# Attention feeding a gated feed-forward on one core: one pair's values moved next to another pair's scores

## The chip, the cores and the metric

The kernel runs on one core of one Trainium2 chip. The metric is the device time of one execution in microseconds (us); where several runs are given, their median stands with the lowest and the highest. A core has five engines, each with its own queue of instructions that it works off in order: TensorE (PE in the rows; PEld is its weight load), VectorE (DVE), ScalarE (ACT), GpSimd (POOL) and SyncE (SP, which here issues the DMAs). TensorE writes its results into PSUM banks of 128 partitions by 512 float32 columns, and VectorE and ScalarE read them from there.

## What is computed

The reference runs attention on 8 batches of 8 heads with 576 positions and 64 features, with a local mask for heads 0 to 3 and a strided mask for heads 4 to 7, and sends the result through a feed-forward without biases:

```python
scores = scale * np.matmul(q, k.transpose(0, 1, 3, 2))
scores = np.where(masks[None, :, :, :], scores, -1000000000.0)
scores = scores - np.max(scores, axis=-1, keepdims=True)
attn = np.exp(scores)
attn = attn / (np.sum(attn, axis=-1, keepdims=True) + 1e-09)
attn_out = np.matmul(attn, v)
x = attn_out.transpose(0, 2, 1, 3).reshape(B * S, H * D)      # 4608 x 512
h = x @ w_in                                                  # 512 x 2048
g = h * (1.0 / (1.0 + np.exp(-1.702 * h)))
return g @ w_out                                              # 2048 x 512
```

The local mask lets a position see the 32 positions up to itself, the strided one the earlier positions with the same remainder modulo 32.

## The kernel before, in words

**Pairs.** The attention of one batch is cut into six pairs (`_pairs`, line 57): three of kind `l` (local heads, 96 queries by 128 keys) and three of kind `s` (strided heads, up to 128 by 108), each pair holding two chunks of four heads. In the batches 1 and 2 they come in the order s, l, s, l, s, l. A pair goes through these steps, each a function that issues one or a few instructions:

- `scores` (line 215, TensorE): 48 small matmuls for `l`, 32 for `s`, into columns 0 to 255 of the two banks `s_banks` (both called `s` in the rows);
- `masked` (VectorE, out of the two banks into SBUF), `maxima` (VectorE), `below` (GpSimd, subtracts the maximum), `exps` (ScalarE), `totals` (VectorE, sum and reciprocal), `scaled` (GpSimd);
- `turn` (line 337): four transposes on TensorE into the first of the two banks, and one ScalarE copy, `kept`, to SBUF;
- `values` (line 341, TensorE): 48 or 32 small matmuls with the values, into the two banks from column `at` on (192 columns for `l`, 180 or 216 for `s`), and then `moves_of`/`moved` (ScalarE copies out of the two banks into the blocks of x: one per bank for `l`, two per bank for `s`);
- `load_qk` and `load_v` (SyncE) fetch the inputs of the pair two further on into the buffer that the pair has just left.

**Passes.** The first product (x times w_in) is done batch by batch. Pass 0 (batch 0) uses plain products: 64 units of six 128-column matmuls over 288 columns. From pass 1 on it uses seven products per weight block in place of eight (a Strassen-like scheme: `product`, `combine`, with sums of x blocks, `x_sum`, and of weight blocks, `t_sum`). Every float32 operand is split into a high and a low part (`x_high`/`x_low`, `w_high`/`w_low_part`, `t_high`/`t_low`), so a unit or product is six matmuls. In pass 0 the w_in blocks are also unpacked (`w_scale`, `w_low`, `w_high` on ScalarE, `w_join` and `w_low_part` on VectorE); in pass 1 the sums of weight blocks are made (`t_load` by DMA, `t_sum` on GpSimd, `t_high` on ScalarE, `t_low` on VectorE). After pass 7 the second product follows.

**Slots.** All order is written out by hand. The main loop counts slots; each slot holds one unit or product on TensorE (two where `product` of two blocks meet), and then whatever was put into that slot with `side(slot, function, ...)` (line 684). Functions of one slot run in the order in which they were registered. Every engine keeps program order, so the slot numbers fix the order of every queue; waits between engines follow from the data. `HEAD` is 61 (where pass 1 begins, `first(1)`), and a pass is 56 slots.

**The attention beside passes 0 and 1.** While pass b runs (b = 0 or 1), the six pairs of batch b+1 are spread over its slots (lines 742 to 752). Pair i begins at slot s = first(b) - 3b + 7i + 2 for b = 0 and without the 2 for b = 1, that is at 2, 9, 16, 23, 30, 37 and at 58, 65, 72, 79, 86, 93. Its `scores` and `masked` stand at s, `maxima` at s+1, `below` at s+2, and the other steps at s plus the entries of `t`:

```python
t = ((4, 5, 6, 11, 12) if b else (2, 3, 3, 10, 12)) if not i else (5, 6, 7, 10, 12)
# exps, totals, scaled, turn, values
```

So the values of pair i stand at s+12, two slots ahead of the scores of pair i+2 at s+14. From pass 2 on (`groups_of`) two pairs go together: the scores of both are written side by side into the two banks before the first of them is read, and so are the values of both.

**Weight sums for pass 1.** Lines 766 to 773 place the steps of weight block i relative to `HEAD`: for block 1 `t_sum` at slot 59, `t_high` at 65, `t_low` at 67. Block 1's sums are first used by the product in slot 70.

Of the kernel before, what the change touches and what calls it, by code (L numbers as in the profile page):

```python
# [31 lines left out]
PAIRS = 6  # L32
# [32 lines left out]
def _size(kind):  # L65

    return (QL, KL) if kind == "l" else (QS, KS)
# [3 lines left out]
def attn_ffn(ctx, tc, qk, vs, weights, masks, ident, out):  # L71
# [81 lines left out]
    s_banks = [psum.tile([P, 512], F32, name=f"s{j}") for j in range(2)]  # L153
# [8 lines left out]
    for j in (1, 2, 3, 0, 4, 5):  # L162
# [3 lines left out]
        t = prs[j].rearrange("p (i m) -> p i m", i=4)  # L166
# [34 lines left out]
    def windows(kind):  # L201

        if kind == "l":
            return [(BL * w, BL, BL * w, WL) for w in range(3)]
        return [(64 * w, 64, WS * w, WS) for w in range(2)]
# [135 lines left out]
    def values(p, banks, at=0):  # L341

        kind, b, c = pairs[p]
        nq = _size(kind)[0]
        v, pt = vts[p], pts[p % 2]
        n0 = QL if kind == "l" else RES[c] * NPOS
        for g in range(2):
            for w, (q0, n, _, nk) in enumerate(windows(kind)):
                if kind == "s":
                    n = min(n0, (w + 1) * WS) - w * WS  # L350
                for u in range(U):
                    i = U * g + u
                    o = g * n0 + (q0 if kind == "l" else w * WS)
                    for j in range(2):
                        slot = j ^ u
                        rows = slice(slot * D, slot * D + nk)
                        matmul(
                            banks[u][j * D : (j + 1) * D, at + o : at + o + n],
                            lhsT=v[rows, i, w, :], rhs=pt[rows, i * nq + q0 : i * nq + q0 + n],
                            start=True, stop=True,  # L360
                        )
        return lambda u, *how: moved(p, u, banks[u][:, at : at + 2 * n0], *how)

    def moves_of(moves):
        for u in range(U):
            for move in moves:
                move(u)

    def moved(p, u, src, copy=scalar.copy, some=(0, 1)):
        kind, _, c = pairs[p]  # L370
        x = {k: xr[k].rearrange("p (g n) -> p g n", g=2) for k in ("11", "12", "21", "22")}
        src = src.rearrange("p (g n) -> p g n", g=2)
        if kind == "l":
            h, o = divmod(c + u, 3)
            copy(out=x[("11", "21")[h]][:, :, o * QL : (o + 1) * QL], in_=src)
            return
        n, r0, half = RES[c], R0[c + u], NPOS // 2
        src = src.rearrange("p g (r t) -> p g t r", r=n)
        for k in some:
            o = x[("12", "22")[k]].rearrange("p g (t r) -> p g t r", r=STRIDE)[:, :, :, r0 : r0 + n]  # L380
            copy(out=o, in_=src[:, :, k * half : (k + 1) * half])
# [235 lines left out]
    def move(i, second, engine):  # L617
        copy = vector.tensor_copy if engine is vector else scalar.copy
        if pairs[i][0] == "l":
            moves[i](second, copy)  # L620
        else:
            for u in range(2):
                moves[i](u, copy, (second,))
# [60 lines left out]
    def side(s, f, *a):  # L684
        sides.setdefault(s, []).append((f, a))

    def first(b):
        return HEAD + PASS * (b - 1) if b else 0
# [16 lines left out]
    def groups_of(b, slots):  # L705

        for g in range(3):
            q, s, then = b * PAIRS + 2 * g, slots[g] + 3 * (g > 0), slots[g + 1]
            side(s, both_scores, q)
            for i in range(2):  # L710
                s += 2 * i * (g == 0)
                side(s + i, masked, q + i, s_banks, 256 * i)
                for f, d in (
                    (maxima, 0), (below, 0), (exps, 4), (totals, 5 + (i and g > 0)),
                    (scaled, 5 + (i and g > 0)),
                ):
                    side(s + d + i, f, q + i, s_banks)
                side(then - (3 - (g > 0), 1)[i], turn, q + i, s_banks[i])
            side(then, both_values, q)

    for b in range(B):
        at = first(b)
        if b == 1:
            for t, f, k in ((-11, x_sum, 1), (-10, x_sum, 3), (-9, x_sum, 2), (-6, x_high, 1),
                            (-5, x_low, 1), (-5, x_high, 4), (-4, x_low, 4), (-3, x_high, 0),
                            (-2, x_low, 0), (-1, x_high, 2), (0, x_low, 2), (1, x_sum, 4),
                            (2, x_high, 3), (3, x_low, 3), (4, x_high, 6), (5, x_low, 6),
                            (6, x_high, 5), (7, x_low, 5)):
                side(at + t, f, k, b)
        elif b:  # L730
            c = b == 2
            side(at - 10 - c, x_sum, 1, b)
            side(at - 9 - c, x_sum, 3, b)
            for k in range(7):
                t = at + 2 * k - 6 + (k == 1)
                side(t, x_high, k, b)
                side(t + 1, x_low, k, b)
            side(at - 4, x_sum, 2, b)
            side(at, x_sum, 4, b)
        if 1 < b < B - 1:  # L740
            groups_of(b + 1, [at + t for t in (3, 16, 30, 44)])
        for i in range(PAIRS if b < 2 else 0):
            p = (b + 1) * PAIRS + i
            s = at - 3 * b + 7 * i + 2 * (not b)
            t = ((4, 5, 6, 11, 12) if b else (2, 3, 3, 10, 12)) if not i else (5, 6, 7, 10, 12)
            side(s, scores, p, s_banks)
            side(s, load_qk, p + 2)
            for f, d in ((masked, 0), (maxima, 1), (below, 2), (exps, t[0]), (totals, t[1]), (scaled, t[2])):
                side(s + d, f, p, s_banks)
            side(s + t[3], turn, p, s_banks[0])  # L750
            side(s + t[4], lambda p=p: moves_of([values(p, s_banks)]))
            side(s + t[4], load_v, p + 2)

    def word(f, i):
        f(raws[i])
# [9 lines left out]
            side(at + t, f, i)  # L765
    for i in range(FP):
        load = -15 + i if i < 3 else 7 * i - 20
        sums, high, low = (-12, -4, -1) if not i else (7 * i - 10 + t + (i == 1) for t in (0, 6, 8))
        for m in range(4):
            side(HEAD + sums + (2 if i > 1 and m > 1 else 0), t_sum, i, m)  # L770
        for t, f in ((load, t_load), (high, t_high), (low, t_low)):
            side(HEAD + t, f, i)
# [241 lines left out]
    for n in range(SETS * NB):  # L1014
        s, q = divmod(n, NB)
# [126 lines left out]
```

## Time and profile before

| | before |
|---|---|
| median of 3 runs | 831.76 us (831.07 to 832.25) |
| the profiled execution, its own time | 831.36 us |
| its span, first to last instruction | 829.3 us |
| TensorE busy | 818.5 us (99%) |
| VectorE busy | 591.7 us (71%) |
| ScalarE busy | 416.3 us (50%) |
| GpSimd busy | 500.3 us (60%) |
| chain that ended last: TensorE's share | 82% |

The profiled execution took 2.06 us more than its span, and lies 0.40 us under the median of the runs. In the timeline a row is a start time in us from the span's start, a length in us, the engine, the operation with the tiles that it writes and reads, the shape, and the number of instructions merged into the row; in square brackets stands how long the engine sat idle before it and what it waited for. `arena` is the one large SBUF tile in which most blocks lie, `mx`, `my`, `mz` are the six product banks, `s` the two attention banks. Matmuls are pipelined: a row's length reaches into the next row, so the cost of a group is read from its start to the next group's start.

### The profile page before, as it was taken

How to read it: one execution, taken by the hardware profiler on the slowest of the kernel's cores; microseconds unless marked ns; L12 is line 12 of the kernel's file. 1: busy time of each engine (PE TensorE's matmuls, PEld its weight loads, DVE VectorE, ACT ScalarE, POOL GpSimd, SP SyncE). 2: the span in 40 equal slices, each digit the busy share in tenths (PEclk: the TensorE clock that was granted, in tenths of full speed). 3: DMA queues.
4: the chain of work that ended last, by engine and by line, in shares of the span. 5: the costliest groups of instructions: out<-in, count | busy, mean ns of one | idle time of the engine just before them, and what ended most of it. 6: DMA issues, size and time to landing. Idle time of an engine off the chain costs nothing.

```text
span 829.3 us, 22486 instructions
## 1 busy us (share of the span) xinstructions
PE 818.5 (99%) x9037; PEld 762.1 (92%) x9037; DVE 591.7 (71%) x998; ACT 416.3 (50%) x642; POOL 500.3 (60%) x507
## 2 busy tenths in 40 slices
PE   7999999999999999999999999999999999999998
PEld 5899999999999999999999998889888888898898
DVE  5776877866767658567667876777767776777774
ACT  4666644534444444343446566555555555555550
POOL 4322886433442433233445359999999888888880
DMA  9898775685776775866678954444444444444431
GB/s 340 308 402 314 223 247 182 193 279 191 234 234 198 240 245 173 274 201 225 212 240 245 301 179 127 128 150 131 150 147 134 151 131 132 147 129 127 128 106 48
DMA packets 112504, 164.74 MB, mean 199 GB/s; under 512 B 9744, under 2 KB 88336, under 8 KB 111504
## 3 DMA queue, kind: packets, MB, share of 16 engines
q1 hardware_dynamic: 112400, 163.31, 60.1%
q8 instruction: 71, 1.16, 0.6%
q14 instruction: 33, 0.27, 0.1%
HBM read 104.55 MB, written 58.72 MB: 197 GB/s over the span
## 4 chain that ended last, share of the span: by engine, by line
PE 82%; DVE 2%; POOL 2%; DMA 1%; issue 1%; ACT 1%; SPq 0%; POOLq 0%; DVEq 0%; ACTq 0%
PE my L87 26%; PE mx L87 22%; PE mz L87 20%; PE s L87 14%; POOL arena L87 2%; DMA arena<-stash 1%; DVE arena L87 1%; DVE xa L87 1%; ACT xa L87 0%; DVE ga L87 0%; DVE w L87 0%; SPq L87 0%; ACT arena L87 0%; DVE w_out L87 0%; POOLq L87 0%
## 5 line engine op out<-in xcount | busy, mean ns | idle before, releaser
L87 POOL TENSOR_TENSOR arena<-arena 128x256 f32<-128x256 f32 (+1 forms) x298 | 331.2, 1128 | 119.0 <-ACT arena L87 39.2
L87 DVE TENSOR_TENSOR xa<-arena,xa 128x576 fp32r<-128x576 f32 (+3 forms) x101 | 152.3, 1511 | 42.0 <-ACT xa L87 37.2
L87 PE MATMUL my<-xa,w 128*128 128x288 f32 x1128 | 180.5, 301 | 0.7 <-DVE w L87 0.4
L87 ACT CAST xa<-arena 128x576 fp32r<-128x576 f32 (+3 forms) x103 | 115.3, 1140 | 90.3 <-POOL arena L87 29.4
L87 PEld LDWEIGHTS my<-xa,w 128*128 128x128 f32 x1128 | 156.2, 188 | 3.7 <-DVE w L87 1.0
L87 DVE TENSOR_TENSOR arena<-my,arena 128x288 f32<-128x288 f32 (+1 forms) x224 | 97.6, 443 | 59.1 <-PE my L87 56.3
L87 ACT COPY arena<-mx 128x288 f32<-128x288 f32 (+3 forms) x163 | 55.8, 364 | 158.9 <-PE mx L87 100.4
L87 PE MATMUL mz<-xa,w 128*128 128x288 f32 x804 | 129.9, 298 | 0.0
L87 PE MATMUL mx<-xa,w 128*128 128x288 f32 x804 | 129.6, 298 | 0.0
L87 ACT ACTIVATE arena<-arena 128x1024 f32<-128x1024 f32 (+2 forms) x120 | 105.3, 877 | 41.5 <-POOL arena L87 19.6
L87 POOL TENSOR_TENSOR arena<-arena,nmax 128x432 f32<-128x432 f32 (+1 forms) x42 | 48.2, 1149 | 110.1 <-DVE nmax L87 102.5
L87 PEld LDWEIGHTS mx<-xa,w 128*128 128x128 f32 x804 | 112.9, 188 | 1.0 <-POOL xa L87 0.2
L87 PEld LDWEIGHTS mz<-xa,w 128*128 128x128 f32 x804 | 113.1, 188 | 0.5
L87 DVE TENSOR_TENSOR arena<-mz,arena 128x288 f32<-128x288 f32 (+1 forms) x168 | 73.8, 442 | 37.0 <-PE mz L87 33.0
L87 POOL TENSOR_TENSOR arena<-arena,rinv 96x512 f32<-96x512 f32 (+1 forms) x48 | 51.2, 1067 | 60.9 <-DVE rinv L87 40.8
L87 PE MATMUL mx<-w_out,xa 128*128 128x512 f32 (+1 forms) x378 | 72.2, 317 | 0.0
L87 PE MATMUL mz<-w_out,xa 128*128 128x512 f32 (+1 forms) x366 | 71.4, 321 | 0.0
L87 PE MATMUL my<-w_out,xa 128*128 128x512 f32 (+1 forms) x366 | 71.3, 320 | 0.0
L87 DVE TENSOR_TENSOR ga<-arena,ga 128x1792 fp32r<-128x1792 f32 (+1 forms) x25 | 55.2, 2209 | 20.4 <-ACT ga L87 16.5
L87 PE MATMUL s<-w_out,xa 128*128 128x512 f32 (+1 forms) x378 | 67.7, 321 | 0.0
L87 ACT CAST ga<-arena 128x1792 fp32r<-128x1792 f32 (+1 forms) x25 | 40.8, 1632 | 44.2 <-POOL arena L87 16.0
L87 PEld LDWEIGHTS s<-w_out,xa 128*128 128x128 f32 x378 | 54.9, 188 | 5.8
(81 smaller groups left out, 1092.0 us busy)
## 6 DMA issues: line engine op xcount, KB each, us to landing
hid<-arena SPq DMA_DIRECT2D x256, 144.0 KB, 3.2
arena<-hid SPq DMA_DIRECT2D x144, 256.0 KB, 3.3
arena<-qk SPq DMA_DIRECT2D x23, 448.0 KB, 5.0
arena<-qk SPq DMA_DIRECT2D x21, 472.0 KB, 5.7
arena<-vs SPq DMA_DIRECT2D x23, 384.0 KB, 4.3
out<-arena SPq DMA_DIRECT2D x34, 256.0 KB, 3.6
stage<-w_out SPq DMA_DIRECT2D x16, 512.0 KB, 4.3
raw<-w_in SPq DMA_DIRECT2D x7, 1024.0 KB, 8.9
```

Of the source, the lines that this page charges most:

```text
L87: ins = call(*args, **kw)
```

## The change

The values of the first four pairs of each of the two passes go from s+12 to s+14, the slot in which the scores of pair i+2 stand, and write the columns from 256 on instead of those from 0 on; `load_v` of the pair two further on goes along. As the list of slot s+14 got the values first, the order there is: values of pair i on TensorE, the ScalarE copies of these values, `load_v`, then the scores of pair i+2. The last two pairs of each pass keep s+12 (they also write from column 256 on).

Beside this, four groups of entries move. In pass 0 the first pair's `turn` goes one slot later (12 to 13). In pass 0 the last pair's `exps`, `totals` and `scaled` go from slots 42, 43, 44 to 41, 42, 42. In pass 1 the first pair's `totals` goes one slot later (63 to 64). For weight block 1 `t_sum` stays at slot 59, `t_high` goes from 65 to 61 and `t_low` from 67 to 64.

```diff
             s = at - 3 * b + 7 * i + 2 * (not b)
-            t = ((4, 5, 6, 11, 12) if b else (2, 3, 3, 10, 12)) if not i else (5, 6, 7, 10, 12)
+            t = ((4, 6, 6, 11, 12) if b else (2, 3, 3, 11, 12)) if not i else (4, 5, 5, 10, 12) if i == PAIRS - 1 and not b else (5, 6, 7, 10, 12)
             side(s, scores, p, s_banks)
             side(s, load_qk, p + 2)
...
             side(s + t[3], turn, p, s_banks[0])
-            side(s + t[4], lambda p=p: moves_of([values(p, s_banks)]))
-            side(s + t[4], load_v, p + 2)
+            then = s + t[4] + 2 * (i < 4)
+            side(then, lambda p=p: moves_of([values(p, s_banks, 256)]))
+            side(then, load_v, p + 2)
...
-        sums, high, low = (-12, -4, -1) if not i else (7 * i - 10 + t + (i == 1) for t in (0, 6, 8))
+        sums, high, low = ((-12, -4, -1), (-2, 0, 3))[i] if i < 2 else (7 * i - 10 + t for t in (0, 6, 8))
```

## Rows read from the trace of the kernel before

**Rows 1.** The page's busy line: time, share of the span, instructions.

```profile
PE 818.5 (99%) x9037; PEld 762.1 (92%) x9037; DVE 591.7 (71%) x998; ACT 416.3 (50%) x642; POOL 500.3 (60%) x507
```

**Rows 2.** Timeline of TensorE in pass 0, slots 21 to 25 (start, length, what).

```profile
47.96 0.90 PE L87 MATMUL s<-arena 64*64 64x32 f32 x48
48.79 1.06 PE L87 MATMUL my<-xa,w 128*128 128x288 f32 x6
49.69 0.95 PE L87 MATMUL mz<-xa,w 128*128 128x288 f32 x6
50.57 0.74 PE L87 MATMUL s<-arena 64*32 64x64 f32 x48
51.23 1.06 PE L87 MATMUL mx<-xa,w 128*128 128x288 f32 x6
52.13 0.95 PE L87 MATMUL my<-xa,w 128*128 128x288 f32 x6
52.92 0.95 PE L87 MATMUL mx<-xa,w 128*128 128x288 f32 x6
```

**Rows 3.** Timeline of TensorE's weight loads: rows with an idle time before them.

```profile
38.19 0.42 PEld L87 LDWEIGHTS s<-ident_sb,arena 128*128 128x128 f32 x4 [0.63 <-POOL arena L87]
...
76.53 0.36 PEld L87 LDWEIGHTS s<-ident_sb,arena 96*128 96x128 f32 x4 [0.70 <-POOL arena L87]
...
95.08 0.69 PEld L87 LDWEIGHTS my<-xa,w 128*128 128x128 f32 x5 [0.35 <-DVE xa L87]
98.69 0.56 PEld L87 LDWEIGHTS my<-xa,w 128*128 128x128 f32 x4 [0.64 <-DVE w L87]
...
101.81 0.56 PEld L87 LDWEIGHTS s<-arena 64*64 64x64 f32 x32 [0.16 <-issue]
```

**Rows 4.** Timeline of TensorE in pass 1: values of kind s, values of kind l.

```profile
99.42 0.69 PE L87 MATMUL s<-arena 54*64 54x54 f32 x32
100.03 1.06 PE L87 MATMUL my<-xa,w 128*128 128x288 f32 x6
...
106.94 0.90 PE L87 MATMUL s<-arena 64*64 64x32 f32 x48
```

**Rows 5.** Timeline of ScalarE: the copies that follow the values of rows 4.

```profile
100.14 0.71 ACT L87 COPY arena<-s 128x108 f32<-128x108 f32 x4 [1.50 <-PE s L87]
...
107.88 0.54 ACT L87 COPY arena<-s 128x192 f32<-128x192 f32 x2 [1.96 <-PE s L87]
```

**Rows 6.** Timeline of TensorE: the scores in slot 16 of pass 0.

```profile
42.79 0.69 PE L87 MATMUL s<-arena 64*64 64x54 f32 x32
```

**Rows 7.** Timeline of ScalarE in pass 0, slots 12 to 14.

```profile
38.93 0.59 ACT L87 COPY arena<-s 128x512 f32<-128x512 f32 x1 [1.39 <-PE s L87]
...
41.70 0.72 ACT L87 COPY arena<-s 128x108 f32<-128x108 f32 x4
...
42.80 1.16 ACT L87 ACTIVATE raw<-raw 128x1024 uint32<-128x1024 uint8 x1
```

**Rows 8.** Timeline of VectorE: w_join of slot 9; x_low of slot 64; t_low of block 1.

```profile
37.81 1.41 DVE L87 SCALAR_TENSOR_TENSOR raw<-raw 128x1024 uint32<-128x1024 uint32 x1
...
94.32 0.71 DVE L87 TENSOR_TENSOR xa<-arena,xa 128x576 fp32r<-128x576 f32 x1
...
97.43 1.21 DVE L87 TENSOR_TENSOR w<-sums,w 128x1024 fp32r<-128x1024 f32 x1
```

**Rows 9.** Timeline of GpSimd in pass 1, slots 64 to 67.

```profile
94.55 1.26 POOL L87 TENSOR_TENSOR arena<-arena,rinv 128x432 f32<-128x432 f32 x1 [1.88 <-ACT arena L87]
95.76 4.13 POOL L87 TENSOR_TENSOR sums<-sums 128x256 f32<-128x256 f32 x2
...
100.86 1.53 POOL L87 TENSOR_TENSOR sums<-sums 128x256 f32<-128x256 f32 x2
```

**Rows 10.** Timeline of ScalarE in pass 1, slots 71 and 72.

```profile
102.43 1.05 ACT L87 CAST w<-sums 128x1024 fp32r<-128x1024 f32 x1 [0.87 <-POOL sums L87]
103.39 0.39 ACT L87 COPY arena<-mx 128x288 f32<-128x288 f32 x1
```

## The prediction, made before the changed kernel ran

> **What bounds the kernel now.** I read the page's busy line first: TensorE is busy 818.5 us of the span, and every other engine under three quarters of it [rows 1]. So a microsecond that TensorE loses or wins in the passes 0 and 1 moves the end by about as much, and the question is what happens on TensorE's own line. There I read the timeline of the stretch that is edited. Between two plain groups the starts lie 0.79 us apart (52.13 to 52.92). A stretch of small attention matmuls breaks this twice: the group ahead of it takes 0.88 (49.69 to 50.57) and the group behind it 0.90 (51.23 to 52.13), so each separate stretch costs 0.09 + 0.11 = 0.20 us beside its own length, which is 0.83 for the values of kind l (47.96 to 48.79) and 0.66 for the scores (50.57 to 51.23) [rows 2]; 0.61 for the values of kind s (99.42 to 100.03) [rows 4]. Last, the weight loads that waited: TensorE stood at two `turn`s for GpSimd (slot 12 at 38.19, slot 47 at 76.53) and at two products for VectorE (slot 67 at 95.08, slot 70 at 98.69); the ordinary gap ahead of an attention stretch is 0.16 [rows 3].
>
> **The change part by part, and what it costs.** Sums are made against the profiled execution, 831.36 us, which lies 0.40 under the median of the runs shown; that difference is left alone.
>
> *Merging.* Eight values stretches (four pairs, two passes) lose their own entry and exit: 8 x 0.20 = -1.60 us. This is certain in itself: whatever happens between values and scores, TensorE goes to small matmuls once instead of twice.
>
> *The small moves.* `turn` one slot later in pass 0: the wait of 0.63 less the ordinary 0.16 goes, -0.47. The last pair's `exps`, `totals`, `scaled` earlier: the wait at 76.53 goes, 0.70 - 0.16 = -0.54; the weight unpacking that ScalarE and VectorE then do later is first used many slots on. In pass 1 `totals` goes behind the `x_low` of slot 64, which then runs earlier by about `totals`' length, so the 0.35 at 95.08 goes. `t_low` of block 1 three slots earlier removes the 0.64 at 98.69 [rows 3]. Sum -2.00. What these make late: the 0.71 us `x_low` now stands ahead of `totals`, and the 1.21 us `t_low` ahead of the next `masked` [rows 8], so `scaled` of slot 64 starts 0.7 later, and GpSimd with it; that is priced below, since it matters only there. `t_high` at slot 61 falls into a stretch in which ScalarE otherwise waits for GpSimd: 0.
>
> *`load_v` two slots later.* It is passed by a few stores and loads on SyncE's queue, it still waits only for the values, as before, and its buffer is next needed 14 slots (some 11 us at 0.79) later: 0.
>
> *The new wait.* This is where the sign is decided. In slot s+14 TensorE writes the values into columns from 256 on of the two banks, ScalarE copies them out, and the next TensorE instruction, the first score, writes columns 0 to 255 of the same two banks. Must it wait for the copies? Before the change two slots of products lay between, so the question never came up. The trace has no row in which TensorE writes one half of a bank while another engine reads the other half; wherever the kernel puts two pairs side by side in a bank (passes 2 and on), all matmuls into it come ahead of the first read. So the price lies between nothing and the full length of the copies. I take the full wait, because in all rows here a bank is written, read and written again in turns, as one tile `s` [rows 2, 4, 5], and column offsets alone are no evidence that the order is kept by columns.
>
> The Trainium skill (PSUM — Partial Sum Buffer, section "PSUM bank collisions raise a hardware error") says that two engines must be kept apart by bank and group of 32 partitions, not by address, and that disjoint columns of one bank still collide. By that the scores wait for the copies, as in my sum; without it the sum would end at the first rival's time. No run here shows it yet.
>
> Its least length, with ScalarE free: the copies begin 0.72 after the start of s values (99.42 to 100.14) and take 0.71, so the scores can start 1.43 after the values instead of 0.61: 0.82 us. For l they begin 0.94 after it (106.94 to 107.88) and take 0.54: 1.48 against 0.83, 0.65 us [rows 2, 4, 5]. Behind the waiting matmul stands all of TensorE's queue. Less the 0.20 for merging, a merge costs +0.62 (s) or +0.45 (l).
>
> *Where ScalarE is not free, pass 0, slot 16 (s).* ScalarE's queue ahead of the copies holds `w_high`, `kept`, `w_scale`, a product copy, `exps` and `w_low`. Before, this block ran from 38.93 to 42.80 + 1.16 = 43.96, with the old copies (0.72) in it [rows 7]: 4.31 without them. `w_high` now stands first and waits for `w_join`, which ends at 37.81 + 1.41 = 39.22 [rows 8], so the copies start at 43.53 and end at 44.25. The scores were at 42.79 [rows 6]; net +1.46 (0.47 and 0.20 already taken off: unwaited they would start at 42.12, so the wait is 2.13).
>
> *The other three of pass 0* (l, s, l): 0.45 + 0.62 + 0.45 = +1.52 at the least. The same `w_scale` and `w_low` stand ahead of them, but with the products that are now ahead of the values there is more time to work them off; if each were as bad as slot 16, 3 x (2.13 - 0.82) = 3.9 more. Nearest to free: I take +0.4.
>
> *Pass 1, slot 72 (s).* Ahead of the copies ScalarE has `t_high` of block 2 (slot 71), which waits for GpSimd's sums: before, 102.43 with 0.87 of waiting [rows 10], and no one on TensorE cared. Now TensorE waits through the copies for `t_high`, and so for GpSimd. GpSimd's block ran from 94.55 to 100.86 + 1.53 = 102.39 [rows 9] and shifts by the 0.71 of `x_low`: 103.10. Then `t_high` 1.05, a copy 0.39 [rows 10], the copies 0.71: 105.25, against scores at 101.81 [rows 3]: +3.44 net. The other bound: two of the sums took 4.13 and the two others 1.53 [rows 9]; if the first two ran as fast, 2.60 less: +0.84. The sums still run beside nearly the same VectorE work, with `t_low` taken out: nearer to the upper end, +2.70. (0.20, 0.35 and 0.64 are in these, as both ends go by GpSimd.) *The other three of pass 1*: GpSimd and ScalarE have caught up during that stall: +1.52.
>
> *Sum:* 1.46 + 1.52 + 0.40 - 0.54 + 2.70 + 1.52 = +7.06; 831.36 + 7.06 = 838.4 us. Later passes keep their order, and start later by as much.
>
> **Rivals.** *First, the other side: no wait.* If the order between engines goes by columns, the scores follow the values at once at all eight places, and what is left is -1.60 - 2.00 = -3.60: 827.8 us. It decides at one point, the gap between the last value and the first score in slot 16. For it: the offset 256 keeps the two column ranges apart, and the copies precede the scores only in the list. Against it: above. This is also the case in which the change does what it says, one stretch; in my forecast the stretch is cut in two by a wait.
>
> *Second, the wait at its least everywhere.* ScalarE's queue is worked off in time at slots 16 and 72 too. Then 8 merges are 4 x 0.62 + 4 x 0.45 = 4.28, and -2.00: 833.6 us. For it: ScalarE is busy only half of the span [rows 1]. Against: the two queues above are in program order, and their lengths come from rows.
>
> *Third, ScalarE late at all of pass 0.* The full 3.9 in place of 0.4, and 3.44 in place of 2.70: +11.3, 842.7 us. For it: the same weight unpacking recurs every seven slots. Against: two more products lie ahead.
>
> **How the numbers follow.** The forecast (wait by bank, long at slots 16 and 72) gets 0.72, with a range of its own from 836 to 841.5; no wait 0.12; least wait 0.08; late everywhere 0.05; 0.03 for effects that cancel within 0.2%. The range that holds the time 8 times in 10 reaches from 833.5, under the second rival, to 841.8, short of the third. About 0.2% (1.7 us) is what a measurement of this kernel can tell from no change: faster 0.12, same 0.03, slower 0.85.
>
> **What would show it.** Right: in the eight slots TensorE idles between values and scores, released by ScalarE, about 0.65 to 0.8 us in most, over 2 at 42 us and some 3 to 5 near 101 us, there with `t_high` waiting for GpSimd ahead of the copies; the four waits of TensorE named above are gone. Wrong: score matmuls that start within 0.1 us of the last value while ScalarE still copies (then the first rival), or idle times of one length (then the second). A time above 842 would mean that a wait was passed on to later slots, which I don't expect since later passes had no wait on TensorE to add to.

## The result, and the profile after

The changed kernel takes 840.5 us (median of 4 runs, 840.19 to 841.06), against 831.65 us for the kernel before in the same session (4 runs, 831.07 to 832.25): ratio 1.010, 95% interval 1.0085 to 1.0116. It is slower by 8.85 us. The prediction was 838.4, with a range from 833.5 to 841.8.

The profiled execution took 841.06 us with a span of 839.0, against 831.36 and 829.3 before: +9.70 us in both. From the page of the changed kernel, the busy line (compare [rows 1]) and the granted clock in 40 slices of some 21 us:

```profile
PE 820.9 (98%) x9032; PEld 765.5 (91%) x9037; DVE 593.0 (71%) x998; ACT 417.2 (50%) x642; POOL 498.1 (59%) x507
PEclk9999989999999999999999999999999999999999
```

TensorE's busy time grew by 2.4 us only; most of what the span gained is idle time of TensorE. And there is a dent in the clock in one slice. Where both came from is read off TensorE's own line, at instructions that both kernels have (start of the same instruction in both traces; "step" is the growth since the line above):

| at | before | after | shift | step | predicted |
|---|---|---|---|---|---|
| scores of slot 2 | 30.92 | 31.30 | +0.38 | +0.38 | 0 |
| group behind the scores of slot 16 | 43.41 | 45.33 | +1.92 | +1.54 | +1.46 |
| group behind the scores of slot 37 | 66.65 | 70.03 | +3.38 | +1.46 | +1.92 |
| values of slot 49 | 78.62 | 81.31 | +2.69 | -0.69 | -0.54 |
| scores of slot 65 | 93.10 | 96.17 | +3.07 | +0.38 | 0 |
| scores of slot 72 | 101.81 | 107.54 | +5.73 | +2.66 | +2.70 |
| group behind the scores of slot 79 | 110.22 | 119.43 | +9.21 | +3.48 | +0.45 |
| values of slot 105 | 136.92 | 147.23 | +10.31 | +1.10 | +1.07 |
| end of the span | 829.3 | 839.0 | +9.70 | -0.61 | 0 |

The last step comes from the later passes, where the shift stays between 10.1 and 10.4 up to 426 us, and where a wait of 0.4 us that the kernel before has, for VectorE's `ga` near 519 us, does not occur.

The weight loads of TensorE that waited in the changed kernel (compare [rows 3]); the brackets give the idle time ahead of the instruction and who ended it:

```profile
42.45 0.57 PEld L87 LDWEIGHTS mz<-xa,w 128*128 128x128 f32 x4 [1.42 <-DVE w L87]
...
44.41 0.86 PEld L87 LDWEIGHTS s<-arena 64*64 64x64 f32 x32 [0.67 <-ACT arena L87]
52.72 0.77 PEld L87 LDWEIGHTS s<-arena 64*32 64x32 f32 x48 [0.52 <-ACT arena L87]
60.89 0.81 PEld L87 LDWEIGHTS s<-arena 64*64 64x64 f32 x32 [0.59 <-ACT arena L87]
69.17 0.77 PEld L87 LDWEIGHTS s<-arena 64*32 64x32 f32 x48 [0.52 <-ACT arena L87]
...
92.15 0.69 PEld L87 LDWEIGHTS mx<-xa,w 128*128 128x128 f32 x5 [0.35 <-DVE xa L87]
...
100.40 0.42 PEld L87 LDWEIGHTS s<-ident_sb,arena 128*128 128x128 f32 x4 [0.36 <-POOL arena L87]
102.17 0.19 PEld L87 LDWEIGHTS my<-xa,w 128*128 128x128 f32 x1 [0.56 <-ACT arena L87]
102.77 0.70 PEld L87 LDWEIGHTS my<-xa,w 128*128 128x128 f32 x5 [0.41 <-DVE xa L87]
...
107.54 1.24 PEld L87 LDWEIGHTS s<-arena 64*64 64x64 f32 x32 [2.56 <-ACT arena L87]
118.57 0.77 PEld L87 LDWEIGHTS s<-arena 64*32 64x32 f32 x48 [0.52 <-ACT arena L87]
126.83 0.81 PEld L87 LDWEIGHTS s<-arena 64*64 64x64 f32 x32 [0.67 <-ACT arena L87]
135.10 0.77 PEld L87 LDWEIGHTS s<-arena 64*32 64x32 f32 x48 [0.52 <-ACT arena L87]
```

Eight times the scores wait for ScalarE between the values and themselves, once for 2.56 us. The `turn`s of slots 13 and 47 and the products of slots 67 and 70 wait no longer. In their place others do: the product of slot 16, at 42.45, stands 1.42 us for `w_low_part` of VectorE, and there are waits at the product of slot 61 (92.15), the `turn` of slot 69 (100.40) and the product of slot 71 (102.17 and 102.77).

Two stretches of ScalarE's queue: the copies of the values of slot 16, and the queue ahead of the long wait (compare [rows 7] and [rows 10]):

```profile
43.96 0.71 ACT L87 COPY arena<-s 128x108 f32<-128x108 f32 x4
...
104.35 0.64 ACT L87 ACTIVATE arena<-arena 96x512 f32<-96x512 f32 x1 [2.66 <-POOL arena L87]
105.84 1.04 ACT L87 CAST w<-sums 128x1024 fp32r<-128x1024 f32 x1 [0.86 <-POOL sums L87]
...
107.09 0.71 ACT L87 COPY arena<-s 128x108 f32<-128x108 f32 x4
```

The values were written from 104.42 on, but their copies stand behind `exps` and `t_high`, which both waited for GpSimd. The copies end at 107.80; the scores start at 107.54 already, 0.26 earlier, which fits with the first of the two banks being free by then. TensorE after that wait, and the same stretch in windows (columns: busy time of the five engines, granted clock, share of DMA, GB/s):

```profile
104.42 0.69 PE L87 MATMUL s<-arena 54*64 54x54 f32 x32
107.54 1.42 PE L87 MATMUL s<-arena 64*64 64x54 f32 x32 [2.44 <-ACT arena L87]
108.89 1.81 PE L87 MATMUL mz<-xa,w 128*128 128x288 f32 x6
110.50 1.64 PE L87 MATMUL my<-xa,w 128*128 128x288 f32 x6
111.94 1.64 PE L87 MATMUL mx<-xa,w 128*128 128x288 f32 x6
```

```profile
104.00:108.00 4.00, 1.56 (x43) 1.25 (x44) 1.09 (x3) 2.58 (x7) 3.57 (x6) 0.89 0.65 201
108.00:112.00 4.00, 4.00 (x43) 3.90 (x44) 1.94 (x5) 0.00 (x0) 0.77 (x2) 0.50 0.70 217
112.00:116.00 4.00, 4.00 (x27) 3.98 (x27) 1.79 (x4) 2.21 (x4) 3.03 (x3) 0.76 0.13 47
```

The groups of products behind the wait start 1.61 and 1.44 us apart, where [rows 2] have 0.79 and 0.90: the granted clock is 0.50 there, which is the 1.2 GHz level. A row of this page that says "busy" does not say at which clock: in the window from 108 TensorE is busy all of its 4 us and does half the work.

### The profile page after: what moved, and what is told of

It reads as the page before. It is cut to its first block, busy times and chain, and to the rows that moved or that the text cites. A ratio compares the mean times of both kernels' runs of the same rounds, so it can differ in the third digit from the quotient of the medians.

```text
span 839.0 us, 22485 instructions
## 1 busy us (share of the span) xinstructions
PE 820.9 (98%) x9032; PEld 765.5 (91%) x9037; DVE 593.0 (71%) x998; ACT 417.2 (50%) x642; POOL 498.1 (59%) x507
## 4 chain that ended last, share of the span: by engine, by line
PE 84%; ACT 0%; DVE 0%; issue 0%
PE my L87 26%; PE mx L87 22%; PE mz L87 21%; PE s L87 15%; ACT arena L87 0%; DVE arena L87 0%
## 5 line engine op out<-in xcount | busy, mean ns | idle before, releaser
L87 POOL TENSOR_TENSOR arena<-arena,nmax 128x432 f32<-128x432 f32 (+1 forms) x42 | 50.7, 1208 | 122.4 <-DVE nmax L87 112.6
```

What stands on the lines that cost most here:

```text
L87: ins = call(*args, **kw)
```

## Experiments

Theory: the order between TensorE and the engine that empties a bank is kept by bank, so the scores wait for the copies of the values; the long wait at slot 72 also costs clock. Rivals: the column offset matters; the small moves matter; the time lies elsewhere in the moved values. The first four runs share 17 runs of the kernel before (median 832.26, 830.98 to 833.69), the last three another 17 (832.34, 830.94 to 836.08).

**Values in columns 0.** Edit of the changed kernel:

```
-            side(then, lambda p=p: moves_of([values(p, s_banks, 256)]))
+            side(then, lambda p=p: moves_of([values(p, s_banks, 0)]))
```

> The change with the moved values written from column 0 on in place of column 256, so over the columns that the next scores write; nothing else differs. Theory (the scores wait for the ScalarE copies because both touch the same bank, whatever the columns): the same time as the change, 840.5 us within 0.5, with the same waits of TensorE between values and scores. Rival (the offset of 256 columns buys something, as disjoint columns are ordered more loosely than overlapping ones): slower than the change, by 0.3 us or more at each of eight places, 843 us or above.

Measured: 842.12 us (840.69 to 843.06), ratio 1.0114 (1.0101 to 1.0128), which overlaps with the change's. TensorE's weight loads at slots 16 and 72, and its waits between 28 and 155 us (total, times, longest):

```profile
44.71 1.00 PEld L87 LDWEIGHTS s<-arena 64*64 64x64 f32 x32 [0.67 <-ACT arena L87]
...
109.37 0.85 PEld L87 LDWEIGHTS s<-arena 64*64 64x64 f32 x32 [2.56 <-ACT arena L87]
```

```profile
PE s L87 <- ACT arena L87: 5.6, 8, 2.4
```

The same eight waits to 0.01 us. With overlapping columns the wait must be there; with disjoint ones it is no shorter. So the order is not kept by columns, and the 256 buys nothing. Each of the two banks is one tile of the program, so no run here tells order by bank from order by tile.

The time is 1.6 us above the 840.5 of the theory, and under the 843 of the rival. The trace shows where the profiled execution lost more than the changed kernel's: the clock fell a second time, behind slot 16.

```profile
44.00:48.00 4.00, 3.46 (x53) 3.10 (x46) 2.22 (x6) 1.11 (x6) 1.04 (x1) 0.67 1.08 382
```

From the scores of slot 16 to the values of slot 23 it takes 8.53 us (44.71 to 53.24), in the changed kernel 7.00 (44.41 to 51.41, clock 1.00); behind slot 72 it is 8.52 against 9.73. From the scores of slot 2 to the values of slot 105 that makes 116.27 us (31.59 to 147.86) against 115.93, and the 0.34 between them is the clock's (1.53 less 1.21).

**The copies taken out from between.** ScalarE's copies are put behind the scores and `masked`; VectorE reads one column of each bank where they stood:

```
+            side(s, masked, p, s_banks)
+            if i > 1:
+                side(s, lambda p=p - 2: moves_of([held.pop(p)]))
...
+            if i < 4:
+                side(then, lambda p=p: held.update({p: values(p, s_banks, 256)}))
+                for bank in s_banks:
+                    side(then, lambda x=bank[:, 256:257]: vector.tensor_copy(out=warm, in_=x))
```

> The change with the ScalarE copies of the four moved pairs put behind the scores and masked of the same slot, and in their former place, between values and scores, one VectorE copy of a single column (256) of each of the two banks. Theory (order by bank: the scores wait for whatever reads the bank ahead of them): the scores now wait for VectorE, 0.2 to 0.4 us in each of the eight places, none waits for ScalarE, the 2.56 us wait in slot 72 is gone with the low clock behind it, and the copies in turn wait for masked, which only reads other columns of the bank; 832 to 834 us. Rival (the scores wait for ScalarE's work itself, for instance for its whole queue, not for a reader of the bank): waits on ScalarE stay, 839 us or more.

Measured: 836.7 us (836.26 to 838.59), ratio 1.0056 (1.0043 to 1.0068). Better than the change by nearly half of what it costs, but 2.7 us above the upper end of what was expected. Two weight loads of TensorE, and the first of ScalarE's copies:

```profile
52.39 0.81 PEld L87 LDWEIGHTS s<-arena 64*32 64x32 f32 x48 [0.36 <-DVE warm L87]
...
105.38 0.81 PEld L87 LDWEIGHTS s<-arena 64*64 64x64 f32 x32 [1.04 <-DVE warm L87]
```

```profile
45.81 0.72 ACT L87 COPY arena<-s 128x108 f32<-128x108 f32 x4 [1.58 <-DVE arena L87]
```

TensorE now waits for a read of one column by another engine, though the scores go to none of the columns that are read. Between values and scores no wait for ScalarE is left, and the clock is 1.00 throughout. What the expectation missed: 0.36 to 0.38 us remain in seven places, 1.04 at slot 72, where VectorE comes later to its read, and the 1.41 for `w_low_part` at 42.62 stays. A second thing shows: at seven of the eight places ScalarE stands idle 1.5 to 2.1 us ahead of its copies (columns from 256), until `masked` (columns below 256) by the releaser in the rows: two readers of one bank. To leave nothing at all between values and scores wasn't tried.

**Only the small moves.** The changed kernel with the values where they were before:

```
-            then = s + t[4] + 2 * (i < 4)
-            side(then, lambda p=p: moves_of([values(p, s_banks, 256)]))
+            then = s + t[4]
+            side(then, lambda p=p: moves_of([values(p, s_banks)]))
```

> The values, their columns and load_v as before the change; only the small moves (turn in pass 0, totals in pass 1, exps, totals and scaled of the last pair, t_high and t_low of block 1) are made. Theory of the prediction: their four waits go and nothing else comes, 2.0 us less than before, 829.6 us. Rival (the wait of 1.42 us for VectorE's low weight part that the change shows in slot 16, and the one of 0.36 us for GpSimd in slot 69, are what two of these moves turn into): 1.0 to 1.5 us less than before, 830.2 to 830.7 us.

Measured: 831.43 us (830.68 to 833.72, 12 runs), ratio 0.9993 (0.9985 to 1.0002): by the ratio 0.6 us less, and by the interval from 1.2 less to 0.2 more. The theory's 2.0 lies outside, and of the rival's 1.0 to 1.5 the interval touches only the lower end. TensorE's weight loads:

```profile
42.92 0.56 PEld L87 LDWEIGHTS s<-arena 54*64 54x64 f32 x32 [1.25 <-ACT arena L87]
...
66.75 0.79 PEld L87 LDWEIGHTS s<-arena 64*64 64x64 f32 x48 [1.09 <-ACT arena L87]
```

The old waits at slots 12, 47, 67 and 70 [rows 3] are gone. Four others stand: these two, and two that the changed kernel has as well, at slots 61 and 69 (0.35 at 92.16, 0.36 at 100.40). The first belongs to this experiment alone: `turn` comes a slot later and the values that need it stay where they were, so of the 1.25 some 1.09 (less the ordinary 0.16) don't speak of the change, and neither does that part of the time. The second, at the values of slot 35 (0.21 before, at 63.37), comes from a DMA that ScalarE waits for, as in the last experiment. This execution opened 2.07 us late, at the scores of slot 2; from there to the values of slot 105 it takes 0.64 longer than the kernel before, so without the 1.09 some 0.45 shorter, and without the 0.88 more at slot 35 some 1.33. So this run alone does not settle what the moves are worth; the last two experiments say more.

**TensorE kept at work in the long wait.** Fourteen extra 128x320 matmuls into a free bank, between values and scores of slot 72; their result is used nowhere:

```
+            if b == 1 and not i:
+                side(then, busy, 14)
```

> The change with 14 extra matmuls (128x128 by 320 columns, bfloat16, into a product bank that is free then; about 1.9 us of TensorE work) between values and scores of slot 72, where TensorE waits 2.56 us. Their result is not used. Theory (that idle time makes the clock fall to its lower level, which costs some 2.5 us in the products behind it): the granted clock stays at 1.0, the products after slot 72 start 0.79 us apart instead of 1.44 to 1.61, and the time falls by 2 to 2.8 us to about 838 us although TensorE has more to do. Rival (the products there are slow for another reason, such as what VectorE and GpSimd do beside them): 840.5 to 841.5 us, with the products as slow as in the change.

Measured: 840.28 us (837.71 to 841.36), ratio 1.0087 (1.0072 to 1.0103). TensorE's timeline, and its waits between 424 and 560 us:

```profile
105.25 0.69 PE L87 MATMUL s<-arena 54*64 54x54 f32 x32
105.87 2.08 PE L87 MATMUL mz<-masks_sb 128*128 128x320 bf16 x14
108.38 0.98 PE L87 MATMUL s<-arena 64*64 64x54 f32 x32 [0.43 <-ACT arena L87]
109.29 1.06 PE L87 MATMUL mz<-xa,w 128*128 128x288 f32 x6
110.18 0.95 PE L87 MATMUL my<-xa,w 128*128 128x288 f32 x6
110.97 0.95 PE L87 MATMUL mx<-xa,w 128*128 128x288 f32 x6
```

```profile
PEld mz L87 <- DVE arena L87: 0.9, 1, 0.9
PEld my L87 <- DVE ga L87: 0.5, 1, 0.5
```

The scores still start 3.13 us behind the values (3.12 in the changed kernel), so the gap is as long; but the clock is 1.00 in all three windows from 104 to 116, the groups are 0.89 and 0.79 apart, and from the scores of slot 72 to the values of slot 79 it takes 7.02 us instead of 9.73: 2.71 us are the clock's. The time misses the 838 of the theory: only 0.2 us is left against the change in the medians, 1.1 by the two ratios, whose intervals overlap, and 1.84 against the run with columns 0 on the same chip. The trace shows one reason: this execution is 1.87 us ahead of the changed kernel's at the `turn` of slot 103 (143.33 against 145.20), though it opened 0.81 later, and then stands 0.9 and 0.5 us in two places that the changed kernel passes without waiting. So the clock's price is shown in the stretch; at the end of the kernel, with openings that differ by 2 us between executions, the medians don't settle how much of it is left.

**Slot 72 left as it was.** Only this one pair's values go back:

```
-            then = s + t[4] + 2 * (i < 4)
+            then = s + t[4] + 2 * (i < 4 and not (b and i == 0))
```

> The change, but the first pair of pass 1 keeps its values in slot 70 (columns from 256 on); the other seven pairs stay moved. Theory (this one place costs 3.4 us of waiting for GpSimd through ScalarE, and the fall of the clock behind it 1.5 to 2.7 us more): the wait of 2.56 us is gone, the granted clock stays at 1.0 after it, and the time lies 5 to 6.5 us under the change's, at a ratio of 1.003 to 1.005 to the kernel before. Rival (what waits there is late anyway, and is waited for at the next place, by turn of slot 69 or 75 or by the values of slot 79): at most 3 us under the change, a ratio above 1.006.

Measured: 836.86 us (836.2 to 840.19), ratio 1.0055 (1.0035 to 1.0074); the profiled span is 834.4, 4.6 shorter than the change's. TensorE's weight load at slot 79, and ScalarE's `t_high` ahead of the copies that it waits for:

```profile
113.46 0.77 PEld L87 LDWEIGHTS s<-arena 64*32 64x32 f32 x48 [1.47 <-ACT arena L87]
```

```profile
111.84 1.04 ACT L87 CAST w<-sums 128x1024 fp32r<-128x1024 f32 x1 [0.92 <-POOL sums L87]
```

One of eight merges, with the clock behind it, costs about half of all. The ratio lies between what the theory (at most 1.005) and the rival (above 1.006) asked for, since 0.95 us are passed on: the wait of slot 79 is 1.47 instead of 0.52, as GpSimd and ScalarE, which catch up in the changed kernel while TensorE stands, are late here. The clock is 1.00.

**Only the moved values.** The changed kernel with the small moves taken back:

```
-            t = ((4, 6, 6, 11, 12) if b else (2, 3, 3, 11, 12)) if not i else (4, 5, 5, 10, 12) if i == PAIRS - 1 and not b else (5, 6, 7, 10, 12)
+            t = ((4, 5, 6, 11, 12) if b else (2, 3, 3, 10, 12)) if not i else (5, 6, 7, 10, 12)
...
-        sums, high, low = ((-12, -4, -1), (-2, 0, 3))[i] if i < 2 else (7 * i - 10 + t for t in (0, 6, 8))
+        sums, high, low = (-12, -4, -1) if not i else (7 * i - 10 + t + (i == 1) for t in (0, 6, 8))
```

> The moved values, columns and load_v of the change, with every other entry as before the change (turn, totals, exps and scaled of the last pair, t_sum, t_high, t_low). Theory of the prediction (the small moves are worth 2.0 us in the change): 842.5 us, a ratio of 1.013. Rival (they are worth next to nothing there: turn's wait only moves to the weight part of slot 16, and behind slot 72 everything waits for GpSimd, which starts 0.7 us earlier without the later totals): 840 to 841.5 us, a ratio of 1.009 to 1.012, with a shorter wait in slot 72 than the change's 2.56 us.

Measured: 841.24 us (839.96 to 842.35), ratio 1.0099 (1.0079 to 1.0119): the change without its small moves is the change, as the rival had it. TensorE's weight loads:

```profile
38.45 0.42 PEld L87 LDWEIGHTS s<-ident_sb,arena 128*128 128x128 f32 x4 [0.64 <-POOL arena L87]
42.33 0.56 PEld L87 LDWEIGHTS mz<-xa,w 128*128 128x128 f32 x4 [0.82 <-DVE w L87]
...
101.79 1.37 PEld L87 LDWEIGHTS my<-xa,w 128*128 128x128 f32 x10 [0.64 <-DVE w L87]
...
107.23 1.24 PEld L87 LDWEIGHTS s<-arena 64*64 64x64 f32 x32 [2.56 <-ACT arena L87]
```

The waits at 38.45 and 42.33 together are 1.46; in the changed kernel the first is gone and the second is 1.42. From the scores of slot 2 to the values of slot 105 it takes 115.80 us (31.18 to 146.98), the changed kernel 115.93 (31.30 to 147.23), so the small moves give nothing inside the change. The 2.56 at slot 72 stays to the hundredth, and is not shorter as the rival expected, since the values come as much earlier as their copies. The scores there come 11.04 us behind those of slot 65 (96.19 to 107.23), against 11.37 in the changed kernel and 8.71 before: the merge at slot 72 costs 2.33 there, and the small moves add 0.33.

**Two of the small moves alone.** The kernel before, with the last pair's `exps`, `totals` and `scaled` earlier and `t_high` and `t_low` of block 1 earlier:

```
-            t = ((4, 5, 6, 11, 12) if b else (2, 3, 3, 10, 12)) if not i else (5, 6, 7, 10, 12)
+            t = ((4, 5, 6, 11, 12) if b else (2, 3, 3, 10, 12)) if not i else (4, 5, 5, 10, 12) if i == PAIRS - 1 and not b else (5, 6, 7, 10, 12)
...
-        sums, high, low = (-12, -4, -1) if not i else (7 * i - 10 + t + (i == 1) for t in (0, 6, 8))
+        sums, high, low = ((-12, -4, -1), (-2, 0, 3))[i] if i < 2 else (7 * i - 10 + t for t in (0, 6, 8))
```

> The kernel before with two of the small moves alone: exps, totals and scaled of the last pair of pass 0 earlier, t_high and t_low of block 1 earlier. Theory (these two remove waits of TensorE without putting another in their place, while later turn and later totals only trade one wait for another): TensorE's waits in slots 47 and 70 are gone, and 0.6 to 1.2 us less than before, a ratio of 0.9985 to 0.9993. Rival (the time won in slot 47 is lost again where pass 1 begins, on the weight sums that come by DMA): within 0.4 us of before.

Measured: 832.41 us (831.3 to 834.85, 12 runs), ratio 0.9999 (0.9988 to 1.0011). No gain, and none in the trace: 106.05 us from the scores of slot 2 to the values of slot 105 (32.30 to 138.35), against 106.00 before. TensorE's weight loads:

```profile
65.21 0.79 PEld L87 LDWEIGHTS s<-arena 64*64 64x64 f32 x48 [0.64 <-ACT arena L87]
90.61 0.69 PEld L87 LDWEIGHTS mx<-xa,w 128*128 128x128 f32 x5 [0.35 <-DVE xa L87]
...
101.62 0.69 PEld L87 LDWEIGHTS my<-xa,w 128*128 128x128 f32 x5 [0.48 <-DVE xa L87]
```

The old waits at slots 47 and 70 are gone, 1.18 in all (0.70 less 0.16, and 0.64); the last two of these rows, at slots 61 and 71, take 0.83 of it back. The first row, at slot 35, stands ahead of everything that this edit moves (slot 41 is the first), so it is not put there by the moves. It waits for `kept` behind `w_high` on ScalarE, and that for a DMA; here and before:

```profile
63.74 1.05 ACT L87 CAST w<-raw 128x1024 fp32r<-128x1024 f32 x1 [3.31 <-DMA plains<-raw]
```

```profile
61.90 1.05 ACT L87 CAST w<-raw 128x1024 fp32r<-128x1024 f32 x1 [2.90 <-DMA plains<-raw]
```

Without the 0.43 that it has more than before (0.64 against 0.21) this execution would be 0.38 shorter than the kernel before, which twelve runs can't tell from nothing. The rival's time came; its reason, the weight sums that come by DMA, accounts at most for the 0.35 at slot 61: `t_high` of block 0 stands 1.41 us for GpSimd's sums there (1.01 before), and `x_high` behind it.

None of the seven is faster than the kernel before by more than its measurement is uncertain.

## Why the prediction was right, and where it was off

The mechanism that decides the sign was right: TensorE waits for the copies at all eight places. The size was 2.1 us short in the medians (838.4 against 840.5), as a clock that falls behind the longest wait was not in the sum; step by step:

**The new wait: right, and shown.** Eight waits between values and scores, released by ScalarE, and none by columns: the run with columns 0 has the same ones. The Trainium skill (PSUM — Partial Sum Buffer, section "PSUM bank collisions raise a hardware error") says that disjoint columns of one bank still collide between engines; the waits of both runs agree with that order (0.52 to 2.56 us). Whether the chip itself would object without it, no run here shows: what the traces have is the wait of the program.

**Slot 72: right in place, in size partly by luck.** +2.66 against +2.70, and by the queue that was predicted: the copies behind `t_high`, that behind GpSimd's sums. GpSimd in the changed kernel (compare [rows 9]):

```profile
98.62 1.73 POOL L87 TENSOR_TENSOR arena<-arena,rinv 128x432 f32<-128x432 f32 x1 [2.86 <-DVE rinv L87]
100.31 3.00 POOL L87 TENSOR_TENSOR sums<-sums 128x256 f32<-128x256 f32 x2
...
104.28 1.53 POOL L87 TENSOR_TENSOR sums<-sums 128x256 f32<-128x256 f32 x2
```

The upper bound, 3.44, had GpSimd 0.71 later and the scores behind the end of the copies; 0.74 was taken off it for sums that run faster. In the trace GpSimd's sums end 9.64 us behind the scores of slot 65 (105.81 less 96.17), 9.29 before (102.39 less 93.10): 0.35 later, not 0.71. That is the balance of three parts: `scaled` starts 1.00 later (2.45 behind those scores, 1.45 before) and takes 0.47 longer, and the first two sums take 3.00 instead of 4.13. So the sums did run faster, by 1.13, but against a later start than forecast. And the scores start 1.73 behind the sums, not 2.15, as the rows of ScalarE's queue overlap a little and the scores don't wait for the end of the copies. 3.44 - 0.36 - 0.42 = 2.66. That these parts come to what a choice between two bounds had taken off is luck. The idle time in the row is 2.56, under the "3 to 5" that it named: TensorE had by then waited itself, at the `turn` of slot 69 and the product of slot 71 (0.36, 0.56 and 0.41).

**Slot 16: right in sum, wrong in kind.** +1.54 against +1.46. ScalarE's queue came out as worked out: copies that end at 44.25, and 0.38 of the opening, make 44.63; the row has 43.96 + 0.71 = 44.67. But the wait is not one of 2.13 for ScalarE: 1.42 of it is ahead of the values, for VectorE's `w_low_part`, and 0.67 behind them. The prediction did not follow VectorE's queue, where `w_low_part` had been covered by the wait at `turn` and by the values that stood ahead of the product: with `turn` in its old place and only the values moved, 0.82 of the 1.42 is there.

**The other six: right.** 1.46 in pass 0 against 1.52 (the 0.40 on top did not come); in pass 1 1.10 for two and, by the like one in pass 0, 0.43 for the third, against 1.52. Each is made up of two parts that were not foreseen: the scores start 1.31 behind l values (51.41 to 52.72) and not 1.48, and then take 0.86 (52.72 to 53.58) and not 0.66; that they wait inside for the second bank fits with it, but no row shows it by itself.

**The small moves, -2.00: wrong.** Taken out of the change they cost nothing (1.0099 against 1.010, and 115.80 us against 115.93 for the stretch), and two of them on the kernel before gain nothing that twelve runs can show. All of them alone give 0.6 us by the ratio (1.2 less to 0.2 more), with 1.09 lost at slot 14 in that run only. The failed step is "the wait goes, less 0.16": the prediction asked what is late next for the moved instructions, not for the consumers behind the wait. The four waits are gone, and in the changed kernel 1.42 at slot 16, 0.35 at 61, 0.36 at 69 and 0.56 and 0.41 at 71 stand instead. Only -0.69 at slot 49 came as forecast (-0.54), and 0.38 of it went again at slot 61, where `x_high` waits behind `t_high` of block 0. As the queues of ScalarE and GpSimd set the steps at slots 16 and 72 anyway, little of this error reached the sum.

**The merging, -1.60:** not measured by itself; it is inside the steps above.

**The clock: missing.** Of the 3.48 us up to slot 79, 2.71 are the clock after the long wait, as the filled wait shows; the other 0.77 stand in that run too (0.43 the merge, the rest mostly the longer scores of slot 72, 0.91 instead of 0.62). That is the term by which the sum (+7.06 against +9.70) fell short, together with 0.38 at the opening, which lies in the spread of executions, and 0.38 at slot 61; a later gain of 0.61 and the 0.46 less at the merges of pass 0 go the other way.

## What to carry to other kernels

Before a producer is put next to another user of the same PSUM bank, look at what lies between: two slots of products had hidden the emptying of the bank, and disjoint columns do not replace them. Follow then the queue of the engine that empties it, back to whatever that engine waits for; this found the place of the longest wait, and bounds for its size, before it was there. And a short wait on the engine that bounds the kernel is worth its length only if the next consumers of the same chain have slack: read their start against their inputs' ends before counting it as gained.

## What was not expected of the hardware

A wait of 2.4 us on TensorE (1.56 us of work between 104 and 108) was followed by a granted clock of 0.50 from 108 to 112 and 0.76 from 112 to 116, though TensorE was busy in all of these 8 us. It cost 2.7 us in the profiled execution of the change, and 1.5 in that with columns 0 (8.52 us for the stretch, clock 0.78 and 0.80); in that of the moved values alone it fell too (0.50 and 0.78). Kept at work with unused matmuls, the clock stayed at 1.00. A shorter wait may do it or not: in the run with columns 0 the two at slot 16 (1.41 ahead of the product, 0.67 ahead of the scores) were followed by a clock of 0.67 from 44 to 48, and cost 1.5; in the changed kernel the same two (1.42 and 0.67) were followed by 1.00.

The clock of the opening differs between executions: 0.83 over the first 30 us in the run of the small moves, 0.89 in that of the moved values alone, 1.00 in the kernel before and the changed one. The first of these had its scores of slot 2 some 2.1 us later than the kernel before (32.99 against 30.92), but the clock does not account for such shifts alone: at 0.89 they start at 31.18, and in two runs with 1.00 at 32.11 and 32.30. A difference under 2 us between single executions of this kernel says nothing; the intervals over 12 runs do.

Two engines that only read one bank seem to be kept in order too: ScalarE's copies started only when VectorE's `masked` released them, after 1.5 to 2.1 us of idle time at seven places, in the run with the copies taken out. No run takes the two to different banks, so this is read off the releaser alone.
